# Mean and scale of seven token tiles, by DRAM and ScalarE in place of TensorE

## The chip, the cores and the metric

The kernel runs on one core of a Trainium2 chip. The metric is the device time of one execution in microseconds. Before the change it is 1456.57 us, the median of three runs (1456.12 to 1456.83).

Five engines work side by side, each through its own instructions in order: TensorE (PE in the profile; PEld is its weight load), VectorE (DVE), ScalarE (ACT), GpSimd (POOL), and SyncE (SP), which issues most of the DMAs. An engine that waits for a semaphore holds up everything behind it in its own queue.

## The reference

The input x is 2048 tokens of 576 features. It is normalized (layer norm without weights), and the normalized tokens go through a linear attention of 32 heads of 18 features and through a gated feed-forward part of 4608 features; the two results are multiplied and added to x.

```python
xn = layernorm(x)                                  # (x - mean) / sqrt(var + 1e-5)
q, k, v = heads(xn @ wqkv)
phi = lambda t: where(t > 0, t + 1, exp(t)) + 1e-6
kv, z = einsum("bhsd,bhse->bhde", phi(k), v), einsum("bhsd->bhd", phi(k))
num, den = einsum(phi(q), kv), einsum(phi(q), z) + 1e-6
s = (num / den) @ wo
b = (gelu(xn @ w_gate) * (xn @ w_up)) @ w_down
out = x + s * silu(b)
```

Everything is float32.

## The kernel before, in words

**Words.** A float32 product is made of passes over "words": an operand is held as an upper part (float32 rounded by a ScalarE copy) and a lower part (what is left, a VectorE subtraction), and TensorE multiplies the parts that matter. So every operand costs ScalarE a copy and VectorE a subtraction (`to_operand`).

**Tiles.** The 2048 tokens are 16 tiles of 128. The features of a tile lie across the partitions for the projections, so the tokens lie along a row. Tiles 0 to 3 are transposed on TensorE. For tiles 4 to 15 the host gives x already transposed beside x as it is (`load_x`), and only mean and scale, which are worked out with one token to a partition, have to be brought into rows.

**Mean and scale.** `spread` takes the moments of two tiles (VectorE, with a logarithm and an exponential on ScalarE) and `scales` finishes the scale; the result is a column of 128 numbers, one to a partition. `turn` (line 208) makes rows of them: two transposes on TensorE (L214 in the profile, out `ms`) of a column that is repeated 128 times, so that each of the 128 partitions of a PSUM bank holds the 128 means, and beside them the 128 scales. `normalize` (line 228) subtracts and multiplies on VectorE with these rows as the second operand (`x<-x,ms`, `xf_B<-x,ms`) and calls `to_operand` (`xo_B`). `place` calls `normalize` for these tiles.

**The k and v stage.** `kv_tile(t)` (line 492) does one tile: three projections `x_mm(t, 0..2)` of 14 matmuls each into banks `kv`; `k_post(t, 0)` and `k_post(t, 1)` form phi(k) (`e_k`, `pk`: two VectorE operations each, then an exponential on ScalarE and an addition on GpSimd); `v_post` copies v on ScalarE (`va`) with a column of ones that GpSimd sets. Between them stand the turn and the place of the next tile: after `x_mm(t, 0)` the turn, then `k_post(t, 0)`, `x_mm(t, 1)`, the place, `k_post(t, 1)`. At even tiles `kv_pair(t)` comes behind `x_mm(t, 0)`: the products of phi(k) and v of the two tiles before, added into one PSUM bank (`kv_a`), 40 matmuls in five groups of heads, of which four have 72 columns and the fifth 36.

**The order.** All instructions are pinned to the order in which the program writes them (`keep_in_program_order`), each on its engine. Tiles 0 to 7 come first, then the q projections of the first 1024 tokens (`q_store`, with short pieces of other work between them from the table `behind`), then tiles 8 to 15, then the rest of q (table `ahead`), the attention's output, and last the feed-forward part, which takes most of the span. Among the pieces of other work are the sums `T1` to `T4` of x operands for the feed-forward part, which `form` cuts into words and stores: the fourth stands at the end of tile 9. The statistics of tiles 12 and 13 are worked out at the end of tile 10, those of 14 and 15 at the end of tile 12.

**Buffers.** Small SBUF tiles of 2 KB a partition come from a ring of six (`gl`), PSUM banks from a ring of six (`one`); `pk` and `va` of two tiles fill a ring of four (`h`).

Of the kernel before, what the change touches and what calls it, by code (L numbers as in the profile page):

```python
# [8 lines left out]
F32 = mybir.dt.float32  # L9
# [82 lines left out]
def block_kernel(ctx, tc, x, xe, xt, wq_d, wkv_d, wo, wgu_d, wd_d, out):  # L92
# [32 lines left out]
    def vec(op, *args, **kw):  # L125
        pin(getattr(nc.vector, op)(*args, **kw))  # L126
# [58 lines left out]
    def scales(n0):  # L185

        n, mv, st = mom.pop(n0)
        v, r, c = (st[:, i, 0:n] for i in range(1, 4))
        if n == 1:
            vec("tensor_scalar", c, r, r, -0.5, op0=ALU.mult, op1=ALU.mult)  # L190
            vec("tensor_scalar", c, c, v, 1.5, op0=ALU.mult, op1=ALU.add)
            vec("tensor_scalar", c, c, r, None, op0=ALU.mult)
        else:
            vec("scalar_tensor_tensor", c, r, -0.5, r, op0=ALU.mult, op1=ALU.mult)
            vec("tensor_mul", c, c, v)
            vec("scalar_tensor_tensor", c, c, 1.5, r, op0=ALU.add, op1=ALU.mult)
        for t in range(n):
            scale_of[n0 + t] = mv[:, t, 0:1], c[:, t : t + 1]

    def center(n):  # L200

        if n >= TT:
            return
        xs = xstat[n // 2][:, n % 2]
        m, r = scale_of.pop(n)
        vec("tensor_scalar", xs, xs, m, r, op0=ALU.subtract, op1=ALU.mult)

    def turn(n, new=bank):

        xs = xstat[n // 2][:, n % 2]  # L210
        if n >= TT:
            xts[n] = t = bank(f"ms_{n}")
            for i, v in enumerate(scale_of.pop(n)):
                pin(nc.tensor.transpose(  # L214
                    t[:, i * P : (i + 1) * P], v.to_broadcast([P, P]), ident
                ))
            return
        tiles = [new(f"xt_{n}_{j}") for j in range(2)]
        xts[n] = [t[:, 0 : 3 * P].rearrange("p (k t) -> p k t", k=3) for t in tiles]
        for j in range(2):  # L220
            for k in range(3):
                pin(nc.tensor.transpose(xts[n][j][:, k, :], xs[:, j, k * P : (k + 1) * P], ident))
# [4 lines left out]

    def normalize(n, s, b, c):

        ms = xts.pop(n)  # L230
        xs = xstat[n // 2][:, n % 2, D:].rearrange("p (k t) -> p k t", k=6)
        m, r = (ms[:, None, i * P : (i + 1) * P] for i in range(2))
        vec("tensor_sub", xs, xs, m.to_broadcast([P, 6, P]))
        for j, nm in enumerate(BS[b]):
            if nm not in xo[s]:
                xo[s][nm] = big(2 * b + j, [P, 5, TBN], F32R, f"xo_{s}_{nm}")
                new_plain(s, nm)
            vec(
                "tensor_mul", xf[s][nm][:, :, c], xs[:, 3 * j : 3 * j + 3],
                r.to_broadcast([P, 3, P]),  # L240
            )
        for nm in BS[b]:
            to_operand(xo[s][nm], xf[s][nm], c)
# [32 lines left out]
        if last:  # L276
            xts.pop(n)

    mom, scale_of, xts = {}, {}, {}

    def to_operand(o, src, c):
        act(o[:, 0:3, c], src[:, :, c], AF.Copy)
# [9 lines left out]
    def difference(s, i):  # L292
        f = xf[s]
        nm, a, b, o = SUMS[i]
        vec("tensor_sub", f[o], f[a], f[b])
        f[nm] = f[o]
# [96 lines left out]
        act(e, e, AF.Exp, scale=-1.0)  # L393
        pool("tensor_add", o, o, e)

    def kv_mm(t):
        if t == 0:
            acc.append(own_bank("kv_a"))
        pk, va = pks.pop(t), vas.pop(t)
        for gi, wdt in enumerate(WIDTHS):  # L400
            for half in range(2):
                o, cs = kv_out(gi, half)
                mm(
                    o, va[:, 2 * gi + half, 0 : o.shape[0]],
                    pk[:, gi * GW + cs.start : gi * GW + cs.stop],
                    start=(t == 0 and gi == 0), stop=(t == S // P - 1),
                    skip_group_check=True,
                )
# [8 lines left out]
    def x_mm(t, c, js=(0, 1), passes=KV_PASSES):  # L417

        tb, i = divmod(t, TT)
        s, b = divmod(tb, 2)  # L420
        begin = (t, c) not in pkv
        if begin:
            pkv[t, c] = bank(f"kv_{t}_{c}")
        o = pkv[t, c]
        for j in js:
            for n, (wi, xi) in enumerate(passes):
                mm(
                    o[:, 0 : TW[c]], xo[s][BS[b][j]][:, xi, i * P : (i + 1) * P], kv_part(c, j, wi),
                    start=(begin and j == 0 and n == 0), stop=(j == 1 and (wi, xi) == (2, 2)),
                )  # L430
# [61 lines left out]
    def kv_tile(t, mid_=(), end=()):  # L492

        ahead = t % (2 * TT) != 2 * TT - 1
        x_mm(t, 0)
        if t % 2 == 0:
            kv_pair(t)
        if ahead:
            turn(t + 1)
        k_post(t, 0)  # L500
        x_mm(t, 1)
        if ahead:
            place(t + 1)
            save(t + 1)
        run(list(mid_))
        k_post(t, 1)
        v_post(t, 1)
        x_mm(t, 2)
        run(list(end))
        v_post(t, 2)  # L510

    def kv_pair(t):

        for i in (t - 2, t - 1):
            if i in vas:
                kv_mm(i)

    ph, ph_d = {}, {}

# [20 lines left out]
    def q_store(tb, gi):  # L540
        if tb not in ph_d:
            ph_d[tb] = dr.tile([P, NHG, TBN], F32, name=f"phd_{tb}")
        o = gl_tile([P, TBN], f"ph_{tb}_{gi}")
        q_mm(tb, gi, o)
        dma(out=ph_d[tb][:, gi, :], in_=o)
# [929 lines left out]
    def form(nm):  # L1475
        keep(0, nm, build(0, nm, 12))

    def form_apart(nm):
# [11 lines left out]
        dma(out=d[:, 2], in_=last[:, 0].bitcast(F32))  # L1490

    behind = {
        (0, 0): [lambda: kv_pair(N0), lambda: spread(N0, 2), lambda: difference(0, 3)],
        (0, 1): [
            lambda: scales(N0), lambda: form("T1"), lambda: q_store(1, 4),
        ],
        (0, 2): [lambda: form_apart("T3")],
        (0, 3): [lambda: turn(N0)],
        (1, 0): [lambda: place(N0)],
        (1, 1): [lambda: form("T2"), lambda: spread(N0 + 2, 2), lambda: scales(N0 + 2)],  # L1500
    }
    for tb in range(2):
        for gi in range(NHG - 1):
# [1 line left out]
            run(behind.get((tb, gi), []))  # L1505
    for n in range(N0, 2 * N0):
        ends = []
        if n < 2 * N0 - 2:
            ends.append(lambda n=n: center(n + 2) if n == N0 else x_next(n + 2))
        if n == N0 + 1:  # L1510
            ends.append(lambda: form("T4"))
        if n == 2 * N0 - 3:
            ends.append(load_wo)
        if n == 2 * N0 - 2:
            ends.append(make_sel)
        if n == 2 * N0 - 1:
            ends += [lambda i=i: difference(1, i) for i in range(3)]
        kv_tile(n, end=ends)
        if n in (N0, N0 + 2):
            load_x(n + 4, 2)  # L1520
    ahead = {
        (2, 0): [lambda: kv_pair(2 * N0), kv_done, spread_sel, lambda: difference(1, 3)],
        (2, 1): [lambda: kv_wo(4), lambda: q_hold(2, 7, 4)],
        (2, 2): [lambda: kv_wo(0), lambda: kv_wo(1), move_rows],
        (2, 3): [lambda: kv_wo(2), lambda: kv_wo(3)],
        (3, 0): [lambda: den(2), lambda: q_hold(3, 8, 4)],
# [117 lines left out]
```

## Time and profile before

| | |
|---|---|
| median of three runs | 1456.57 us |
| the profiled execution, its own time | 1456.24 us |
| its span in the profile | 1454.5 us |
| instructions | 22180 |
| VectorE busy from 126 to 135 us | 8.11 of 9 us |
| TensorE busy from 126 to 135 us | 8.79 of 9 us |
| L214 (turns), TensorE | 24 instructions |
| wait of GpSimd's `pk` for ScalarE, 85 to 180 us | 44.4 us, 8 times |

The profile is one execution. A row of a timeline gives the start, the duration, the engine, the line, the operation with its output and inputs by name, the count, and in brackets the idle time before it with what ended it. Instructions of one kind that follow each other are merged into one row. L123, L126, L129, L132 and L135 are the helpers through which ScalarE, VectorE, TensorE, GpSimd and SP get nearly all instructions, so the names of the tiles tell them apart. Matmuls are pipelined: their durations overlap, and what one costs is the distance from start to start.

### The profile page before, as it was taken

The numbers are of one execution on the slowest core, as the hardware profiler recorded it, in microseconds if no ns is written. First come the engines' busy times: TensorE is split into PE (matmuls) and PEld (weight loads), VectorE is DVE, ScalarE is ACT, GpSimd is POOL, SyncE is SP. The second block draws the span as 40 slices with busy tenths as digits, with TensorE's granted clock in tenths as the row PEclk, the third lists the DMA queues.
The fourth block names the chain that finished last, engine by engine and source line by source line (L and its number), as shares of the span: only waits on it lengthen the run. The fifth ranks groups of instructions, "written<-read, shape, count | busy, mean of one in ns | idle before, by whom it ended". The sixth has DMA issues, their size and how long they took to land.

```text
span 1454.5 us, 22180 instructions
## 1 busy us (share of the span) xinstructions
PE 1447.7 (100%) x8286; PEld 1289.9 (89%) x8286; DVE 1149.5 (79%) x1605; ACT 561.3 (39%) x914; POOL 579.6 (40%) x520
## 2 busy tenths in 40 slices
PE   9999999999999999999999999999999999999998
PEld 8989989988888888888888888888889999999998
DVE  7787767376787887888777878778888978989888
ACT  6343355332222233322332232332235555545454
POOL 3342340235756567566475755667632000000000
PEclk9999999999999999999999999999999999999999
DMA  5543105521422315224242243323389887767886
GB/s 223 191 190 141 38 30 212 209 109 51 169 98 104 130 51 182 94 94 140 72 159 87 98 149 106 113 85 118 129 277 349 262 263 251 249 188 232 278 289 224
DMA packets 118085, 233.98 MB, mean 161 GB/s; under 512 B 11018, under 2 KB 44682, under 8 KB 116058
## 3 DMA queue, kind: packets, MB, share of 16 engines
q1 hardware_dynamic: 115178, 220.31, 45.0%
q0 software_dynamic: 2656, 12.06, 2.2%
q8 instruction: 65, 1.06, 0.3%
q14 instruction: 42, 0.34, 0.1%
q10 hardware_dynamic: 144, 0.20, 0.0%
HBM read 149.91 MB, written 82.58 MB: 160 GB/s over the span
## 4 chain that ended last, share of the span: by engine, by line
PE 98%; DVE 1%; ACT 0%; issue 0%; POOL 0%; DVEq 0%; ACTq 0%; POOLq 0%
PE bd L129 25%; PE al L859 16%; PE de L859 16%; PE ga L859 16%; PE kv L129 8%; PE be L859 8%; PE s L129 4%; PE q L129 4%; PE kv_a L129 1%; PE idle L129 0%; PE d L129 0%; PE kw L129 0%; PE b L129 0%; PE ms L214 0%; DVE acc L126 0%
## 5 line engine op out<-in xcount | busy, mean ns | idle before, releaser
L132 POOL TENSOR_TENSOR sm<-raw 128x384 f32<-128x384 f32 x72 | 75.2, 1044 | 145.9 <-DMA raw<-in_wgu_dram 120.6
L129 PE MATMUL kv<-wkv,xo_B 128*128 128x412 f32 (+2 forms) x662 | 125.7, 348 | 0.0
L129 PEld LDWEIGHTS kv<-wkv,xo_B 128*128 128x128 f32 x662 | 119.8, 188 | 1.4 <-DVE wkv L126 0.5
L126 DVE TENSOR_TENSOR wa<-sm,wa 128x768 fp32r<-128x768 f32 x72 | 92.3, 1282 | 36.1 <-ACT wa L123 35.2
L129 PE MATMUL bd<-w_head,hi 128*128 128x288 f32 x516 | 117.9, 294 | 0.0
L126 DVE TENSOR_TENSOR wb<-raw,wb 128x256 fp32r<-128x256 f32 (+1 forms) x108 | 102.1, 946 | 7.4 <-ACT wb L123 5.8
L126 DVE TENSOR_TENSOR wa<-raw,wa 128x256 fp32r<-128x256 f32 x72 | 66.3, 921 | 51.7 <-ACT wa L123 50.6
L123 ACT ACTIVATE hi<-raw_h 128x1024 fp32r<-128x1024 f32 x59 | 62.5, 1060 | 94.8 <-PE bd L129 64.8
L129 PE MATMUL bd<-w_end,hi 128*128 128x288 f32 x448 | 89.8, 294 | 0.0
L123 ACT ACTIVATE spot_h<-spot_h 128x512 f32<-128x512 f32 x49 | 30.7, 633 | 150.3 <-DVE spot_h L126 150.3
L129 PEld LDWEIGHTS bd<-w_head,hi 128*128 128x128 f32 x516 | 87.0, 188 | 0.1
L126 DVE TENSOR_TENSOR raw_h<-raw_h,hi 128x1024 fp32r<-128x1024 f32 x59 | 71.7, 1220 | 17.3 <-ACT hi L123 17.2
L129 PE MATMUL bd<-w_end,raw_h 128*128 128x288 f32 x264 | 77.9, 295 | 0.0
L123 ACT ACTIVATE wa<-sm 128x1152 fp32r<-128x1152 f32 x36 | 41.8, 1161 | 91.8 <-PE de L859 91.8
L123 ACT ACTIVATE u<-al 128x512 f32<-128x512 f32 x72 | 40.9, 593 | 89.5 <-PE al L859 56.3
L129 PEld LDWEIGHTS bd<-w_end,hi 128*128 128x128 f32 x448 | 71.9, 188 | 0.0
L129 PE MATMUL bd<-beside,raw_h 128*128 128x288 f32 x240 | 70.8, 295 | 0.0
L132 POOL TENSOR_TENSOR spot_h<-spot_h,spot_h 128x512 f32<-128x512 f32 x45 | 62.7, 1399 | 2.9 <-DVE spot_h L126 2.4
L859 PE MATMUL al<-xo_B,wa 128*128 128x512 f32 x252 | 63.0, 389 | 0.0
L859 PE MATMUL al<-xr_B,wa 128*128 128x512 f32 x252 | 63.0, 389 | 0.0
L859 PE MATMUL be<-xo_T,wa 128*128 128x512 f32 x252 | 63.0, 389 | 0.0
L859 PE MATMUL be<-xr_T,wa 128*128 128x512 f32 x252 | 63.0, 389 | 0.0
(274 smaller groups left out, 4039.9 us busy)
## 6 DMA issues: line engine op xcount, KB each, us to landing
raw_h<-hs SPq DMA_DIRECT2D x176, 256.0 KB
raw<-in_wgu_dram SPq DMA_DIRECT2D x36, 768.0 KB
hs<-spot_h SPq DMA_DIRECT2D x90, 256.0 KB
hs<-spot_g SPq DMA_DIRECT2D x80, 256.0 KB
b<-in_wd_dram SPq DMA_DIRECT2D x42, 432.0 KB
hs<-spot_m SPq DMA_DIRECT2D x38, 256.0 KB
raw_g<-hs SPq DMA_DIRECT2D x22, 256.0 KB
raw_a<-hs SPq DMA_DIRECT2D x20, 256.0 KB
```

The source lines that it names most:

```text
L123: pin(nc.scalar.activation(*args, **kw))
L126: pin(getattr(nc.vector, op)(*args, **kw))
L129: pin(nc.tensor.matmul(*args, **kw))
L132: pin(getattr(nc.gpsimd, op)(*args, **kw))
L859: nc.tensor.matmul(o, w[0:rows, wi, :], xop[0:rows, xi, :], start=(start and n == 0), stop=(n == len(PASSES) - 1), skip_group_check=True,)
```

## The change

For tiles 8 to 15 `scales` now also writes the scales and the means of two tiles side by side (four numbers, 16 bytes, to a partition), stores them to DRAM, and loads them back with the whole 2 KB repeated on every partition. `sort_rows`, a ScalarE copy, brings the four numbers of a token into four rows. `normalize` takes the rows from there for tiles 9 to 15; tile 8 still takes them from a turn. Where the rows exist, `kv_tile` places the next tile right after the first projection, ahead of `k_post(t, 0)`, and makes no turn.

Three things go with it. The statistics of tiles 12 and 13 move from the end of tile 10 to the end of tile 9, those of 14 and 15 from the end of 12 to the end of 11, and the fourth form from the end of tile 9 to the end of tile 10. `kv_pair` does the wide groups of both tiles before the narrow group of both. And the q operand of group 4, which reads its small tile from the ring, comes one step earlier, twice.

```diff
@@ scales
+        if n0 >= 2 * TT:
+            vec("tensor_copy", st[:, 3, 2:4], mv[:, 0:2, 0])
+            d = dr.tile([P, 4], F32, name=f"md_{n0}")
+            mixed[n0] = g = gl_tile([P, P, 4], f"mx_{n0}")
+            dma(out=d, in_=st[:, 3, :])
+            dma(
+                out=g.rearrange("p t c -> p (t c)"),
+                in_=d.rearrange("t c -> (t c)")[None, :].to_broadcast([P, 4 * P]),
+            )
+
+    def sort_rows(n0):
+
+        g = gl_tile([P, 4, P], f"mr_{n0}")
+        act(g, mixed.pop(n0).rearrange("p t c -> p c t"), AF.Copy)
+        for t in range(2):
+            if n0 + t > 2 * TT:
+                rows_of[n0 + t] = [g[:, None, i + t] for i in (2, 0)]
@@ turn
+        if n in rows_of:
+            return
@@ normalize
-        ms = xts.pop(n)
+        if n in xts:
+            ms = xts.pop(n)
+            m, r = (ms[:, None, i * P : (i + 1) * P] for i in range(2))
+        else:
+            m, r = rows_of.pop(n)
-        m, r = (ms[:, None, i * P : (i + 1) * P] for i in range(2))
@@ kv_tile
+        early = t + 1 in rows_of
         x_mm(t, 0)
         if t % 2 == 0:
             kv_pair(t)
-        if ahead:
+        if early:
+            place(t + 1)
+        elif ahead:
             turn(t + 1)
         k_post(t, 0)
         x_mm(t, 1)
-        if ahead:
+        if ahead and not early:
             place(t + 1)
             save(t + 1)
         run(list(mid_))
         k_post(t, 1)
         v_post(t, 1)
+        if t + 2 in mixed:
+            sort_rows(t + 2)
         x_mm(t, 2)
@@ kv_pair
-        for i in (t - 2, t - 1):
-            if i in vas:
-                kv_mm(i)
+        pair = [i for i in (t - 2, t - 1) if i in vas]
+        for groups in (range(4), (4,)):
+            for i in pair:
+                kv_mm(i, groups)
+        for i in pair:
+            del pks[i], vas[i]
@@ the order of the work
-        (0, 0): [lambda: kv_pair(N0), lambda: spread(N0, 2), lambda: difference(0, 3)],
-        (0, 1): [
-            lambda: scales(N0), lambda: form("T1"), lambda: q_store(1, 4),
+        (0, 0): [
+            lambda: kv_pair(N0), lambda: q_store(1, 4), lambda: spread(N0, 2),
+            lambda: difference(0, 3),
         ],
+        (0, 1): [lambda: scales(N0), lambda: form("T1")],
...
+        (1, 2): [lambda: sort_rows(N0)],
...
-        if n < 2 * N0 - 2:
-            ends.append(lambda n=n: center(n + 2) if n == N0 else x_next(n + 2))
-        if n == N0 + 1:
+        if n in (N0, N0 + 2):
+            ends.append(lambda n=n: load_x(n + 4, 2))
+        if n in (N0 + 1, N0 + 3):
+            ends.append(lambda n=n: x_next(n + 3))
+        if n == N0 + 2:
             ends.append(lambda: form("T4"))
...
-        if n in (N0, N0 + 2):
-            load_x(n + 4, 2)
...
-        (2, 0): [lambda: kv_pair(2 * N0), kv_done, spread_sel, lambda: difference(1, 3)],
-        (2, 1): [lambda: kv_wo(4), lambda: q_hold(2, 7, 4)],
+        (2, 0): [
+            lambda: kv_pair(2 * N0), kv_done, lambda: q_hold(2, 7, 4), spread_sel,
+            lambda: difference(1, 3),
+        ],
+        (2, 1): [lambda: kv_wo(4)],
```

More of the change, by code (lines that the diff above doesn't have):

```diff
@@ L277, in save @@
             xts.pop(n)
-    mom, scale_of, xts = {}, {}, {}
+    mom, scale_of, xts, rows_of, mixed = {}, {}, {}, {}, {}
     def to_operand(o, src, c):
@@ L394, in phi, with kv_mm @@
         pool("tensor_add", o, o, e)
-    def kv_mm(t):
-        if t == 0:
+    def kv_mm(t, groups):
+        if not acc:
             acc.append(own_bank("kv_a"))
-        pk, va = pks.pop(t), vas.pop(t)
-        for gi, wdt in enumerate(WIDTHS):
+        pk, va = pks[t], vas[t]
+        for gi in groups:
             for half in range(2):
```

## The prediction, made before any run of the changed kernel

> **What bounds the kernel now.** I read the page first, then TensorE's timeline of the stage that the diff touches (85 to 180 us), then the same stretch on VectorE, ScalarE and GpSimd, because a change that takes work from TensorE is worth only what the other engines let it keep.
>
> ```profile
> span 1454.5 us, 22180 instructions
> PE 1447.7 (100%) x8286; PEld 1289.9 (89%) x8286; DVE 1149.5 (79%) x1605; ACT 561.3 (39%) x914; POOL 579.6 (40%) x520
> PE 98%; DVE 1%; ACT 0%; issue 0%; POOL 0%; DVEq 0%; ACTq 0%; POOLq 0%
> ```
>
> TensorE is busy 1447.7 of 1454.5 us and carries 98% of the chain that ended last. So an instruction taken off TensorE shortens the kernel by its issue time, as long as nothing else arrives late. TensorE's timeline around tiles 10 to 14 shows the pairs of turns (L214), the accumulations of two tiles (`kv_a`), and the projections (`kv`):
>
> ```profile
> 125.23 1.38 PE L129 MATMUL kv_a<-pk,va 128*64 128x72 f32 x40
> 126.54 0.32 PE L214 MATMUL ms<-ident,mv 128*128 128x128 f32 x1
> 126.70 0.27 PE L214 MATMUL ms<-ident,st 128*128 128x128 f32 x1
> 126.73 7.95 PE L129 MATMUL kv<-wkv,xo_B 128*128 128x412 f32 x42
> 134.52 0.27 PE L214 MATMUL ms<-ident,mv 128*128 128x128 f32 x1
> 135.54 0.32 PE L214 MATMUL ms<-ident,st 128*128 128x128 f32 x1 [0.76 <-DVE st L126]
> 135.62 7.95 PE L129 MATMUL kv<-wkv,xo_B 128*128 128x412 f32 x42
> 143.50 1.38 PE L129 MATMUL kv_a<-pk,va 128*64 128x72 f32 x40
> ```
>
> A turn between two projections, from the same timeline in a narrower window:
>
> ```profile
> 152.79 0.27 PE L214 MATMUL ms<-ident,mv 128*128 128x128 f32 x1
> 152.90 0.27 PE L214 MATMUL ms<-ident,st 128*128 128x128 f32 x1
> 152.93 0.43 PE L129 MATMUL kv<-wkv,xo_B 128*128 128x412 f32 x1
> ```
>
> Durations overlap here (columns: start, duration, engine, line, operation); what a turn costs is the distance between starts. Within the stage VectorE is nearly as full as TensorE, and its order is what the change rearranges. Its timeline for the last q operand and tile 8:
>
> ```profile
> 110.58 0.69 DVE L126 TENSOR_SCALAR ph<-q 128x512 f32<-128x512 f32 x1 [0.46 <-ACT e_q L123]
> 111.19 0.58 DVE L126 TENSOR_SCALAR e_k<-kv 128x416 f32<-128x416 f32 x1
> 111.68 0.58 DVE L126 TENSOR_SCALAR pk<-kv 128x416 f32<-128x416 f32 x1
> 112.18 0.94 DVE L126 TENSOR_TENSOR x<-x,ms 128x768 f32<-128x768 f32 x1
> 113.16 1.02 DVE L126 TENSOR_TENSOR xf_B<-x,ms 128x384 f32<-128x384 f32 x2
> 114.30 1.51 DVE L126 TENSOR_TENSOR xo_B<-xf_B,xo_B 128x256 fp32r<-128x256 f32 x4
> 115.84 0.32 DVE L126 TENSOR_SCALAR e_k<-kv 128x160 f32<-128x160 f32 x1
> ```
>
> The second k step (160 columns) of tile 9, that of tile 11, and the statistics of tiles 12 and 13 with the instruction that follows them:
>
> ```profile
> 122.23 0.33 DVE L126 TENSOR_SCALAR e_k<-kv 128x160 f32<-128x160 f32 x1
> ```
>
> ```profile
> 140.08 0.33 DVE L126 TENSOR_SCALAR e_k<-kv 128x160 f32<-128x160 f32 x1
> ```
>
> ```profile
> 132.35 0.82 DVE L126 BATCH_NORM_STATS2 bn<-x 128x6 f32<-128x288 f32 x2
> ```
>
> ```profile
> 135.41 0.58 DVE L126 TENSOR_SCALAR e_k<-kv 128x416 f32<-128x416 f32 x1
> ```
>
> From these starts: the first k step takes 1.0 us of VectorE (111.19 to 112.18), the normalization of a tile ("place") 3.66 us (112.18 to 115.84), the mean and scale of two tiles 3.06 us (132.35 to 135.41).
>
> **What is removed.** Seven pairs of turns go, for tiles 9 to 15. One that stands between projections (9, 10, 14) costs the 0.14 us from its first start to the next projection (152.79 to 152.93), and the slower first projection after it.
>
> ```profile
> L129 PE MATMUL kv<-wkv,xo_B 128*128 128x412 f32 x112 | 22.8, 354 | 0.0
> ```
>
> The mean of such a projection is 0.35, against 0.43 here: 0.08 more, 0.22 in all. A turn behind `kv_a` (11, 13, 15) costs 0.19 (126.54 to 126.73), because the slower first projection stays. Tile 12's costs 134.52 to 135.62 and the 0.08, 1.18 us, because the second turn waits 0.76 us for VectorE's scale. The sum is 3 x 0.22 + 3 x 0.19 + 1.18 = 2.4 us. The regrouped `kv_a` enters the narrow groups once in a pair instead of twice; no row shows what one entry costs. I bound it by nothing and by two of a pair's forty instructions (1.38 / 40 = 0.035 each), and take one, 0.03, so 0.2 us in eight pairs. Moving the four transposes of q operand 4 one step earlier moves the same instructions: nothing. If nobody is late, TensorE gains **2.65 us**.
>
> **What is added.** Four small VectorE copies (nearest rows: `st` operations of 0.16, so 0.1 to 0.2 each), four `sort_rows` copies on ScalarE of 128x512 elements, and on SP four stores of 2 KB and four loads of 256 KB. The load waits on SP for the store to land, and later SP work queues behind it. Its other entries in this stage are stores and x loads, and no wait quoted here ends with one of these, so I put SP at nothing.
>
> A transfer of 256 KB in this kernel, from issue on SP to last packet (slices of 0.2 us from 84.0; the packets lie in slices 13 to 16, so they end by 87.4):
>
> ```profile
> 85.79 4.67 SPq L135 DMA_DIRECT2D phd<-ph  x2
> ```
>
> ```profile
> GB/s 0 0 0 0 0 82 0 0 0 0 0 0 0 317 399 420 174 0 0 0 0 0 0 0 0 0 0 0 0 0 0 0 0 0 72 358 440 379 62 0
> ```
>
> 1.6 us, so the two in a row take some 3.5 us with the wait between them (an estimate; the nearest row that has a landing time is 4.1 us, of another queue, which makes 8.2).
>
> For `sort_rows` the nearest row is ScalarE's other 512-element pass, 590 ns; at half the rate it would be the 1045 ns of 1024 elements. I take 0.59.
>
> ```profile
> L123 ACT ACTIVATE e_q<-q 128x512 f32<-128x512 f32 x9 | 5.3, 590 | 5.4 <-PE q L129 5.4
> L123 ACT ACTIVATE xo_T<-xf_B 128x1024 fp32r<-128x1024 f32 x1 | 1.0, 1045 | 0.0
> ```
>
> ```profile
> hs<-spot_h POOLq DMA_DIRECT2D x12, 256.0 KB, 4.1
> ```
>
> `sort_rows` reads one word in every 16 bytes, which no ScalarE row here does. The Trainium skill (SBUF — State Buffer, Specifications (TRN2)) says that SBUF has 16-byte lines, that two hits on a line are needed for full bandwidth and that each crossing to a new line costs something; no run shown here bears on it.
>
> **What is moved, and what is late next.** Tile t+1 is now normalized ahead of tile t's k steps. Tile t's `pk` is therefore ready later, since the 3.66 us of a place now stand ahead of all its k steps and not between the first and the second, and `kv_a` of an even tile waits for the `pk` and `va` of the odd tile before it. From the second k step (e_k of 160 columns) to both being ready takes 2.67 us: 115.84 to the end of the memset at 118.51.
>
> ```profile
> 116.26 0.69 ACT L123 ACTIVATE e_k<-e_k 128x576 f32<-128x576 f32 x1 [1.53 <-DVE e_k L126]
> 116.85 0.76 ACT L123 ACTIVATE va<-kv 128x252 f32<-128x252 f32 x3
> ```
>
> ```profile
> 123.50 1.48 ACT L123 ACTIVATE xo_T<-xf_B 128x1536 fp32r<-128x1536 f32 x1
> ```
>
> ```profile
> 125.01 1.92 DVE L126 TENSOR_TENSOR xo_T<-xf_B,xo_T 128x1024 fp32r<-128x1024 f32 x2 [2.23 <-ACT xo_T L123]
> ```
>
> ```profile
> 118.39 0.12 POOL L132 MEMSET va<- 128x10 f32 x1
> ```
>
> A second effect: mean and scale used to be read from PSUM (`ms`); now they come from SBUF, so the subtraction and the two products read SBUF twice. VectorE operations with two SBUF inputs and GpSimd's additions shut each other out in this trace. The second of three equal differences takes 2.88 against 1.76 us, 1.1 more, beside an addition of GpSimd that takes 2.46:
>
> ```profile
> 77.26 1.76 DVE L126 TENSOR_TENSOR xf_B<-xf_B,xf_B 128x1536 f32<-128x1536 f32 x1
> ```
>
> ```profile
> 79.05 2.88 DVE L126 TENSOR_TENSOR xf_B<-xf_B,xf_B 128x1536 f32<-128x1536 f32 x1
> ```
>
> ```profile
> 77.85 2.46 POOL L132 TENSOR_TENSOR pk<-pk,e_k 128x576 f32<-128x576 f32 x1 [0.95 <-ACT e_k L123]
> ```
>
> ```profile
> L126 DVE TENSOR_TENSOR x<-x,ms x12: 941/954/956, 40.0 to 162.6; 128x768 f32<-128x768 f32 x12
> ```
>
> The subtraction from PSUM (last row: shortest, median and longest of twelve, in ns) is never slowed, though the one at 112.18 lies beside GpSimd's addition.
>
> Now the queue, on the clock of before. `sort_rows` of tiles 8 and 9 stands on ScalarE ahead of the e_q that VectorE's 110.58 waits for: 111.1. Place(9) starts at 111.7, meets GpSimd's last `ph` addition (+1.0), and ends at 116.4; TensorE waits some 0.6 us for tile 9's operand, later swallowed. The second k step of tile 8 is at 117.4. ScalarE follows with exponential (117.8), one `va` copy (118.4), `sort_rows` of 10 and 11 (118.75 to 119.35). Place(10) starts at 119.4, loses 0.5 to GpSimd's addition, and the second k step of tile 9 falls at 119.4 + 0.5 + 3.66 + 1.0 = 124.6, against 122.23. Ready at 127.3; TensorE wants tile 9 at 125.3 (125.23 + 0.6 of tile 8, less 0.5 gained). **It idles**, and is then 1.4 us behind before.
>
> Next: the statistics of tile 12, now here, 125.15 to 128.3; place(11) to 132.0; second k step of tile 10 at 133.0; on ScalarE the exponential at 133.4, `va`, `sort_rows` of 12 and 13 at 134.3, the fourth form's upper words 134.9 to 136.3; VectorE's lower words to 138.3 (1.95); place(12) to 141.95; second k step of tile 11 at 142.95 instead of 140.08. Ready at 145.6, where before began tile 11's accumulation at 143.50 + 0.6 = 144.1. So everything gained ahead of this point is lost, and 1.5 us more. Behind it VectorE has slack, and turns 13 to 15 (0.60) and three pairs (0.1) are kept: 1.5 - 0.7 = **+0.8 to 0.9 us**. The profiled execution took 1456.24 (its span and 1.74 around it), 0.33 under the median; on the median that is **1457.4**, its own range 1456.2 to 1458.6 for 0.3 us of error at each of the steps.
>
> **The rivals.**
> - *The full gain.* VectorE isn't late, because some wait that I add up (ScalarE's order, the clash with GpSimd) doesn't come. For it: 2.9 us of the walk are waits, not work. Against it: the margin of tile 11 in before is only 1.35 us (ready 142.75, wanted 144.1), less than the 1.8 us by which TensorE comes sooner. 1456.57 - 2.65 = 1453.9.
> - *No clash.* If operands with a stride of nought leave GpSimd alone, 1.5 us of the walk go and tile 11 is ready at 144.1, as before: the last 0.7 remain, 1455.9.
> - *Sorting at half rate*, each word read by itself: `sort_rows` takes 1.05 instead of 0.59 us, on the path three times, but once covered by the clash: +0.9, so 1458.3. The Trainium skill's rule of lines (SBUF — State Buffer) points this way.
> - *Slower by more: ScalarE held at `sort_rows` of tile 12.* It stands ahead of the fourth form, which stands ahead of place(12). It decides from the point at which store and load take over 6.0 us (128.3 to 134.3); every microsecond beyond is one at `kv_a` of tile 11. At 8.2 us it is +2.2: 1459.6.
> - That the turns stay is excluded: the code returns ahead of them.
>
> **How the numbers follow.** Forecast 0.42, full gain 0.22, no clash 0.15, half rate 0.11, held 0.10. What a measurement can tell from no change is about 0.2%, 2.9 us: below 1453.7 or above 1459.5. The full gain misses that bound narrowly (0.05 beyond it, for error in its sum); of the held case and the forecast's tail 0.10 lie above. So faster 0.05, same 0.85, slower 0.10. The range runs from the full gain, 1453.8, to 1459.0 between half rate and held.
>
> **What would show it.** Right: L214 has 10 turns instead of 24; `kv_a` around 127 and 145 us waits for GpSimd or VectorE; VectorE's subtraction takes over 1.3 us beside GpSimd's additions; the profile's starts around 160 lie some 1 to 1.5 us later than before. Wrong: no idle ahead of `kv_a` (full gain), subtractions of 0.95 throughout (no clash), `sort_rows` near 1 us, or ScalarE waiting for a DMA ahead of it.

## The result, and the profile after the change

The changed kernel takes **1460.58 us** (median of seven executions, 1460.44 to 1464.23) where the kernel before takes 1456.57 on the same chip (seven executions, 1455.94 to 1458.10). The ratio is 1.0033, with a 95% interval from 1.0021 to 1.0045: slower by 4.0 us. The forecast was 1457.4, and its range ended at 1459.0. The execution that was profiled took 1460.58 itself; its span is 4.3 us longer than that of before. Three of the seven executions took 1462.1 to 1464.2 and four 1460.4 to 1460.6; no record here says why.

The page of the changed kernel, its span, its busy times, and the first line of the chain that ended last:

```profile
span 1458.8 us, 22167 instructions
...
PE 1448.0 (99%) x8272; PEld 1289.4 (88%) x8272; DVE 1149.4 (79%) x1609; ACT 566.7 (39%) x918; POOL 579.9 (40%) x520
...
PE 86%; DVE 3%; POOL 1%; DMA 1%; ACT 1%; issue 1%; ACTq 0%; DVEq 0%; SPq 0%; POOLq 0%
```

TensorE issues 14 instructions fewer, as it should (ten of the 24 transposes of L214 are left, which are five turns; where the prediction speaks of 10 and 24 turns it means these instructions), and is busy for the same 1448 us; what grew is its idle time. In the chain it falls from 98% to 86%, because the chain now leaves it for VectorE, GpSimd, ScalarE and the DMAs: it passes through the load of tiles 12 and 13, which ends at about 136 us, and comes back to TensorE at 149.2. The view of waits, TensorE between 85 and 190 us of the changed kernel (in total, how often, the longest):

```profile
PE kv_a L129 <- POOL va L132: 2.6, 2, 1.6
PE kv L129 <- ACT xo_B L123: 1.1, 2, 0.8
PE kv_a L129 <- ACT va L123: 0.7, 2, 0.4
```

Before the change there was one wait in this stage, the 0.76 us of tile 12's turn. Now there are six, of 4.4 us together. TensorE's timeline of the changed kernel shows where:

```profile
115.61 10.65 PE L129 MATMUL kv<-wkv,xo_B 128*128 128x416 f32 x56 [0.81 <-ACT xo_B L123]
126.18 0.72 PE L129 MATMUL kv_a<-pk,va 128*64 128x72 f32 x16
127.90 0.47 PE L129 MATMUL kv_a<-pk,va 128*64 128x72 f32 x8 [0.99 <-POOL va L132]
128.73 0.61 PE L129 MATMUL kv_a<-pk,va 128*64 128x72 f32 x16 [0.37 <-ACT va L123]
...
142.65 2.92 PE L129 MATMUL kv<-wkv,xo_B 128*128 128x416 f32 x14 [0.29 <-ACT xo_B L123]
...
147.84 0.47 PE L129 MATMUL kv_a<-pk,va 128*64 128x72 f32 x8 [1.62 <-POOL va L132]
148.62 0.61 PE L129 MATMUL kv_a<-pk,va 128*64 128x72 f32 x16 [0.31 <-ACT va L123]
149.16 15.67 PE L129 MATMUL kv<-wkv,xo_B 128*128 128x412 f32 x84
```

The first wait is for the operand of tile 9, the fifth row's for that of tile 12. The other four stand inside `kv_a` of the pairs 8/9 and 10/11: 16 matmuls go through, then TensorE waits for the `pk` and `va` of the odd tile, does 8, and waits again, for the last two `va` copies, before the other 16. Behind the last of them the next projections, from the second of tile 12 on, start at 149.16 where they started at 145.00.

VectorE's timeline of the changed kernel, the rows that set these waits:

```profile
111.88 0.69 DVE L126 TENSOR_SCALAR ph<-q 128x512 f32<-128x512 f32 x1 [1.49 <-POOL ph L132]
...
113.47 2.00 DVE L126 TENSOR_TENSOR xf_B<-x,mr 128x384 f32<-128x384 f32 x2
...
118.13 0.31 DVE L126 TENSOR_SCALAR e_k<-kv 128x160 f32<-128x160 f32 x1
...
120.54 1.01 DVE L126 TENSOR_TENSOR x<-x,mr 128x768 f32<-128x768 f32 x1 [1.87 <-ACT mr L123]
...
125.28 0.31 DVE L126 TENSOR_SCALAR e_k<-kv 128x160 f32<-128x160 f32 x1
...
133.66 0.31 DVE L126 TENSOR_SCALAR e_k<-kv 128x160 f32<-128x160 f32 x1
...
138.53 1.92 DVE L126 TENSOR_TENSOR xo_T<-xf_B,xo_T 128x1024 fp32r<-128x1024 f32 x2 [4.33 <-ACT xo_T L123]
140.49 0.96 DVE L126 TENSOR_TENSOR x<-x,mr 128x768 f32<-128x768 f32 x1
...
145.17 0.31 DVE L126 TENSOR_SCALAR e_k<-kv 128x160 f32<-128x160 f32 x1
```

The two products of tile 9 at 113.47 take 2.00 us (1.02 before). The row at 111.88 names GpSimd, whose addition to `ph` had just ended, at 111.82; but the same instruction of VectorE waits for ScalarE's exponential `e_q` before the change and in experiment 2, and here `e_q` comes behind `sort_rows` and ends at 111.79. So this wait too goes back to ScalarE's order. Place(10) waits for the sorted rows (`mr`), and the fourth form's subtraction at 138.53 waits 4.33 us for ScalarE. The second k steps (160 columns) of tiles 8, 9, 10 and 11 start at 118.13, 125.28, 133.66 and 145.17. ScalarE, same kernel:

```profile
110.19 1.11 ACT L123 ACTIVATE mr<-mx 128x512 f32<-128x512 f32 x1
...
127.88 0.30 ACT L123 ACTIVATE st<-mv,eps_t 128x2 f32<-128x2 f32 x1 [1.29 <-DVE mv L126]
...
128.32 0.49 ACT L123 ACTIVATE va<-kv 128x252 f32<-128x252 f32 x2
...
136.01 1.11 ACT L123 ACTIVATE mr<-mx 128x512 f32<-128x512 f32 x1 [0.98 <-DMA mx<-md]
137.02 1.48 ACT L123 ACTIVATE xo_T<-xf_B 128x1536 fp32r<-128x1536 f32 x1
```

`sort_rows` takes 1.11 us, not 0.59, and the one of tiles 12 and 13 waits 0.98 us for its load; the fourth form's copy (137.02) stands behind it. And at 127.88 the logarithm of the statistics waits for VectorE, with two `va` copies behind it. The store and the load of tiles 12 and 13 on SP's queue:

```profile
129.10 0.34 SPq L135 DMA_DIRECT2D md<-st  x1
130.65 0.34 SPq L135 DMA_DIRECT2D mx<-md  x1
```

The load arrives at 136.01, where ScalarE's wait ends: 6.9 us behind the store's issue.

### The profile page after: what moved, and what is told of

Its sections match the earlier page's. It is cut to its first block, busy times and chain, and to the rows that moved or that the text cites. A ratio compares the mean times of both kernels' runs of the same rounds, so it can differ in the third digit from the quotient of the medians.

```text
span 1458.8 us, 22167 instructions
## 1 busy us (share of the span) xinstructions
PE 1448.0 (99%) x8272; PEld 1289.4 (88%) x8272; DVE 1149.4 (79%) x1609; ACT 566.7 (39%) x918; POOL 579.9 (40%) x520
## 4 chain that ended last, share of the span: by engine, by line
PE 86%; DVE 3%; POOL 1%; DMA 1%; ACT 1%; issue 1%; ACTq 0%; DVEq 0%; SPq 0%; POOLq 0%
PE bd L129 25%; PE ga L889 15%; PE de L889 15%; PE al L889 15%; PE be L889 7%; PE s L129 4%; PE kv L129 2%; PE q L129 2%; POOL spot_h L132 0%; DMA hs<-spot_g 0%; DMA mx<-md 0%; PE d L129 0%; PE kw L129 0%; PE b L129 0%; POOL spot_g L132 0%
## 5 line engine op out<-in xcount | busy, mean ns | idle before, releaser
L889 PE MATMUL ga<-xo_B,wb 128*128 128x512 f32 x252 | 63.1, 390 | 0.4 <-DVE u L126 0.4
```

The lines of the kernel that those rows point to most:

```text
L889: nc.tensor.matmul(o, w[0:rows, wi, :], xop[0:rows, xi, :], start=(start and n == 0), stop=(n == len(PASSES) - 1), skip_group_check=True,)
```

## The experiments

**My theory** after the traces: the spreading itself is nearly harmless, and the time goes into three waits on a chain that VectorE and ScalarE share: the place ahead of the k steps, ScalarE's sorting (its length, and its wait for the load) ahead of urgent work, and the last `va` copy behind the statistics. **The rivals**: the clash of VectorE with GpSimd explains most of it; the sorting, by its length, does; or the part of the change that has nothing to do with the rows (the regrouped `kv_a`, the moved q step) does. Differences below are of medians, against the kernel before on the same chip (1457.01 in the first four, 1456.71 in the next four, 1457.00 in the last four); the ratios weigh all executions and can differ from them a little.

### 1. Rows that cost nothing

Nothing is stored, loaded or sorted; the rows are those of a constant.

```diff
-            (the copy, the store and the load)
+            mixed[n0] = None
-                rows_of[n0 + t] = [g[:, None, i + t] for i in (2, 0)]
+                rows_of[n0 + t] = [ident[:, None, :]] * 2
```

> Leaves out the spreading: no copy, no store, no load, no sort_rows; place takes the rows of a constant tile in SBUF, so the output isn't the reference's. The order of the work is that of the changed kernel. Theory (the loss is queueing on ScalarE and VectorE behind sort_rows and its load): sort_rows of 1.11 us is gone three times and the 0.98 us wait for the load with it; the clash with GpSimd stays and so do the statistics ahead of the last va copy, so kv_a still waits a little around 126 and 144 us; about 1456.3, 4 us under the changed kernel. Rival (the regrouped kv_a and the moved pieces cost the time): stays at 1460 to 1461.

Measured: 1456.70, ratio 0.9997 [0.9988, 1.0005], 0.3 under before. Spreading and sorting are worth 4.3 us of the loss. But even rows that cost nothing make nothing faster. TensorE's timeline of this kernel:

```profile
126.33 0.47 PE L129 MATMUL kv_a<-pk,va 128*64 128x72 f32 x8 [0.32 <-POOL va L132]
127.08 0.61 PE L129 MATMUL kv_a<-pk,va 128*64 128x72 f32 x16 [0.29 <-ACT va L123]
...
144.81 0.61 PE L129 MATMUL kv_a<-pk,va 128*64 128x72 f32 x16 [0.28 <-ACT va L123]
```

Three waits are left, of 0.9 us; two end with the `va` copy. So the order and the clash, which are still in this kernel, take back what the removed turns bring, but make no loss by themselves. On VectorE the clash stands as in the changed kernel: 2.01 us for the two products of tile 9, and 2.14 for those of tile 10:

```profile
118.83 2.14 DVE L126 TENSOR_TENSOR xf_B<-x,ident 128x384 f32<-128x384 f32 x2
```

### 2. Sorted rows in PSUM

```diff
-        g = gl_tile([P, 4, P], f"mr_{n0}")
+        g = bank(f"mr_{n0}").rearrange("p (c t) -> p c t", c=4)
```

> sort_rows writes its rows into a PSUM bank, so that VectorE's subtraction and products have one SBUF input. Theory: place of tile 9 loses the 1.0 us that it waits for GpSimd (its two products 1.02 instead of 2.00 us), and the chain behind shifts by as much, to 1459.5. Rival (operands of two SBUF inputs don't matter on the path): 1460.6; a bank that is missed elsewhere: above 1460.6.

Measured: 1460.48, ratio 1.0024 [1.0014, 1.0034], so 0.5 us better than the change against its own runs of before, less than the intervals tell apart. The time is the rival's 1460.6 and not the theory's 1459.5. In the trace the clash is gone: the two products of tile 9 take 1.02 us, and TensorE's longest wait, in the pair 10/11, ends at 146.56 instead of 147.84, 1.3 us earlier. The profiled execution gave that back in another place. Two rows of its TensorE timeline, and a row of the view by stretches (the stretch and its length; busy us and count of PE, PEld, DVE, ACT, POOL; granted clock; DMA share; GB/s):

```profile
146.56 0.47 PE L129 MATMUL kv_a<-pk,va 128*64 128x72 f32 x8 [1.64 <-POOL va L132]
...
148.15 16.98 PE L129 MATMUL kv<-wkv,xo_B 128*128 128x412 f32 x84
```

```profile
148.15:150.90 2.75, 2.75 (x12) 2.67 (x9) 2.53 (x6) 0.99 (x2) 0.00 (x0) 0.50 0.03 1
```

The granted clock is 0.50 for 3.4 us behind the idle time, from 147.5 to 150.9 (the row shows the last 2.75), and the 84 projections take 16.98 us where the changed kernel's take 15.67 (its row at 149.16). The clash is real and its size is as I had it, but it isn't most of the loss.

### 3. Sorting by the store

The store writes the four numbers of a token into four rows of DRAM, 512 packets of 4 bytes, and ScalarE sorts nothing.

```diff
-            d = dr.tile([P, 4], F32, name=f"md_{n0}")
+            d = dr.tile([4, P], F32, name=f"md_{n0}")
-            dma(out=d, in_=st[:, 3, :])
+            dma(out=d.rearrange("c t -> t c"), in_=st[:, 3, :])
```

> The store to DRAM writes the four rows already sorted (512 packets of 4 bytes instead of 128 of 16), the load brings them to every partition, and there is no sort_rows. Theory: ScalarE's 1.11 us goes three times and the fourth form is no longer held by the load, so nearly as e1, 1456.5; place of tile 12 has until about 136 us for its rows. Rival (store and load are the cost, whoever waits): VectorE waits for the load ahead of place, 1459 to 1461.

Measured: 1478.89, ratio 1.0152 [1.0139, 1.0165], 21.9 us slower than before. **Every theory missed.** SP's timeline for the pair of tiles 8 and 9:

```profile
115.78 0.37 SPq L135 DMA_DIRECT2D md<-st  x1
126.07 0.32 SPq L135 DMA_DIRECT2D mr<-md  x1
```

The load waits on SP for the store, and that now takes 10.3 us from the store's issue to the load's. Over the four pairs it takes 8.8 to 10.9 us, where the changed kernel takes 1.5 to 3.0 (1.55 for the pair shown above, from 129.10 to 130.65). The rows come too late at every pair, and the operands with them (waits of TensorE, 85 to 190 us):

```profile
PE kv L129 <- ACT xo_B L123: 12.9, 4, 6.4
```

All waits of TensorE in this stage make 15.2 us of the 21.9. Behind them the granted clock is 0.50 in four stretches, of 20.5 us together, and matmuls there take longer. The run says nothing on ScalarE's sorting, but it shows how steep the loss is once the rows are late.

### 4. The place back between the k steps

```diff
-        if early:
-            place(t + 1)
-        elif ahead:
+        if ahead and not early:
             turn(t + 1)
...
-        if ahead and not early:
+        if ahead:
             place(t + 1)
```

> Place goes back behind the second projection, so that the first k step stands ahead of it on VectorE, as before; the rows still come by DRAM and sort_rows. Theory: the first k step of tile 9 fills VectorE's wait for sort_rows (1.87 us idle ahead of place 10), and the second k steps of tiles 9 and 11 come 1.0 us sooner: 1459.5. Rival (order of place and k steps is the main cause, since a place stands ahead of both k steps): 1457 or less.

Measured: 1459.01, ratio 1.0014 [1.0005, 1.0022], 2.0 over before: half of the loss goes with one move of the order, near the 1459.5 of the theory and not the 1457 of the rival. `kv_a` of the pair 8/9 no longer waits at all; the pair 10/11 still does, for 0.96 us. The place of tile 9 has become the tighter one:

```profile
115.98 10.65 PE L129 MATMUL kv<-wkv,xo_B 128*128 128x416 f32 x56 [1.21 <-ACT xo_B L123]
```

### 5. The last `va` copy of odd tiles ahead of the statistics

```diff
-        run(list(end))
-        v_post(t, 2)
+        if t > 2 * TT and t % 2:
+            v_post(t, 2)
+            run(list(end))
+        else:
+            run(list(end))
+            v_post(t, 2)
```

> The changed kernel, but at tiles 9, 11, 13 and 15 the last va copies stand ahead of the statistics and not behind them. Theory: kv_a of tiles 10 and 12 no longer waits the 0.37 and 0.31 us for va behind the logarithm; about 0.3 to 0.6 us under the changed kernel. Rival (the wait for pk covers it): no difference.

Measured: 1460.21, ratio 1.0023 [1.0014, 1.0032]. That is 0.5 us better than the change, as expected, but less than the intervals tell apart. The two waits for `va` are gone from TensorE's timeline, but a part of it is lost again, since the operand of tile 12 comes later instead (1.00 in place of 0.29):

```profile
142.69 2.91 PE L129 MATMUL kv<-wkv,xo_B 128*128 128x416 f32 x14 [1.00 <-ACT xo_B L123]
```

One wait mended alone is mostly paid at the next.

### 6. The order alone, without the rows

The kernel before, with the regrouped `kv_a` and the q step moved as in the change, and the turns kept.

```diff
+        for groups in (range(4), (4,)):
+            for i in pair:
+                kv_mm(i, groups)
...
+            lambda: kv_pair(N0), lambda: q_store(1, 4), lambda: spread(N0, 2),
```

> The kernel before with two parts of the change alone: the groups of kv_a regrouped, and the q operand of group 4 one step earlier, twice. Theory: 0.2 us faster than before, so no difference that can be measured. Rival (the moved pieces cost the time): 2 us or more slower than before.

Measured: 1457.06, ratio 1.0001 [0.9992, 1.001]: no difference. A pair of `kv_a` goes from 1.38 to 1.36 us. So the rival falls for these two parts. The moved statistics, the moved fourth form and the x loads behind them are not in this run; no run takes them alone.

### 7. Sorting without the stride, a load that doesn't wait

The load takes 128 different rows of x and waits for no store, and ScalarE's copy reads its 512 words in a row.

```diff
-                in_=d.rearrange("t c -> (t c)")[None, :].to_broadcast([P, 4 * P]),
+                in_=x[n0 * P : (n0 + 1) * P, 0 : 4 * P],
...
-        act(g, mixed.pop(n0).rearrange("p t c -> p c t"), AF.Copy)
+        act(g, mixed.pop(n0).rearrange("p t c -> p (t c)").rearrange("p (c t) -> p c t", c=4), AF.Copy)
```

> The changed kernel, but the load of 256 KB takes 128 different rows of x from DRAM in place of one row of 2 KB repeated, so it does not wait for the store, and sort_rows reads its 512 words in a row: other values, so the output isn't the reference's. Theory: packets of the load take about 84 ns as those of the q stores, not 200 to 300; sort_rows takes 0.59 and not 1.11 us; ScalarE doesn't wait ahead of the second-to-last sort_rows; in all some 2 us under the changed kernel. Rival (the 16 bytes are not the reason, and the load is slow for the x load beside it): 1.11 us and 3 us stay.

Measured: 1458.66, ratio 1.0013 [1.0004, 1.0022], 1.95 over before and so 2.1 better than the change. The group of sorting copies in this kernel:

```profile
L123 ACT ACTIVATE mr<-mx 128x512 f32<-128x512 f32 x4 | 2.5, 621 | 0.0
```

621 ns for the same 512 words in a row, where the changed kernel's group has 1115. No copy waits for a DMA. So the length of the sorting and the late load are worth half of the loss while order and clash stay. That doesn't make order and clash the other half: in experiment 1 they stay too, and nothing is lost. What one of the parts costs depends on which others are there.

### 8. All of it mended

The place late again (4), the rows in PSUM (2), the last `va` copy of odd tiles ahead of the statistics (5), and two sortings moved behind the work that they held up:

```diff
-        if t + 2 in mixed:
+        if t + 2 in mixed and t != 2 * TT + 2:
             sort_rows(t + 2)
...
-        (1, 2): [lambda: sort_rows(N0)],
+        (1, 3): [lambda: sort_rows(N0)],
...
-            ends.append(lambda: form("T4"))
+            ends += [lambda: form("T4"), lambda n=n: sort_rows(n + 2)]
```

> The changed kernel with the causes of the theory mended together: place behind the second projection as before, the rows in PSUM, sort_rows of tile 8 behind the last q operand, that of tile 12 behind the fourth form, and the va copies of odd tiles ahead of the statistics. Theory: TensorE waits under 0.5 us at kv_a of tiles 10 and 12, and the gain of 2.65 us less at most 1 us is left: 1.6 to 2.6 us faster than before. Rival (the rows by DRAM can't be had without TensorE waiting): as before or slower.

Measured: **1454.66**, ratio 0.9984 [0.9975, 0.9993], 2.05 us faster than before and 6.1 better than the change. It beats both kernels. One wait of TensorE is left between 85 and 190 us:

```profile
142.79 0.86 PE L129 MATMUL kv_a<-pk,va 128*64 128x72 f32 x24 [0.17 <-POOL va L132]
```

On ScalarE the fourth form comes first, and the sorting of tiles 12 and 13 behind it finds its load there (no wait in brackets). It still takes 1.10 us; it holds nobody now:

```profile
131.84 1.48 ACT L123 ACTIVATE xo_T<-xf_B 128x1536 fp32r<-128x1536 f32 x1
133.21 1.10 ACT L123 ACTIVATE mr<-mx 128x512 f32<-128x512 f32 x1
```

This version and the changed kernel issue the same 8272 matmuls in the same order, so their starts can be laid side by side. The distance grows by 1.0 us at tile 9's operand, by 1.7 in the pair 8/9, 0.6 at tile 12's operand and 1.9 in the pair 10/11 (5.4 in the stage, for the six waits above, with some 0.15 of refilling each), then by 0.7 at 498 us, where a `ga` matmul waits for VectorE. The last also stands in the profile of experiment 6 (0.7), whose time is that of before; I count it to the execution and not to the change.

### 9 to 12. The mended version, with one mend taken back

Each of the four differs from version 8 by one mend (number 12 by two).

```diff
(9)  +        g = gl_tile([P, 4, P], f"mr_{n0}")
(10) +        if early:
     +            place(t + 1)
(11) +        if t + 2 in mixed:
     +            sort_rows(t + 2)
(12) +        run(list(end))
     +        v_post(t, 2)
     +        (1, 2): [lambda: sort_rows(N0)],
```

> The mended version with the rows back in SBUF, all else as there. If the clash between VectorE's operations on two SBUF inputs and GpSimd's additions costs the kernel time by itself, the places of tiles 9 to 12 last some 1.0 us longer and the kernel is 0.5 to 1.0 us slower than the mended version's 2.05 us below the kernel before: 1.05 to 1.55 us below. Rival: with the order mended VectorE has that much slack in this stage and the clash is swallowed: 1.9 to 2.2 below.

> The mended version with the place of the next tile ahead of the k steps again. If the earlier place costs by itself (the second k step 2.7 us later, as the first experiment with the late place had it at 1.6 us of 3.6), the kernel stands 0.4 to 1.0 us below the one before instead of 2.05. Rival: the earlier place only hurt because sorting and the clash came on top of it; then it stays 1.9 to 2.2 below.

> The mended version with the sorting of tile 12 ahead of the fourth form again. If ScalarE's wait for the load (about 1 us) and the 1.1 us of sorting ahead of the fourth form push place(12) and the k steps behind it, the kernel stands 0.3 to 1.0 us below the one before instead of 2.05 (1.1 to 1.8 us lost). Rival: the place of tile 12 comes late enough behind the fourth form to swallow it: 1.9 to 2.2 below.

> The mended version with the last va copy of odd tiles behind the statistics' logarithm again and the sorting of tile 8 back ahead of the last q operand. If the va copy behind the logarithm is a wait of its own at kv_a, 0.3 us at two to three pairs come back: 1.1 to 1.7 us below the kernel before instead of 2.05. Rival: VectorE's order hides both: 1.9 to 2.2 below.

| version | median us | ratio to before, interval | against before | TensorE's waits, 85 to 190 us |
|---|---|---|---|---|
| 8: mended | 1454.66 | 0.9984 [0.9975, 0.9993] | -2.05 | 0.2 |
| 9: rows in SBUF | 1455.47 | 0.9987 [0.9978, 0.9995] | -1.53 | 0.5 |
| 10: place early | 1456.40 | 0.9996 [0.9987, 1.0004] | -0.60 | 1.6 |
| 11: sorting ahead of the fourth form | 1456.66 | 0.9997 [0.9989, 1.0006] | -0.34 | 2.0 |
| 12: `va` last, sorting of tile 8 early | 1456.45 | 0.9995 [0.9986, 1.0004] | -0.55 | 1.3 |
| the change | 1460.58 | 1.0033 [1.0021, 1.0045] | +4.01 | 4.4 |

The intervals of 10, 11 and 12 still overlap that of 8 a little; that these are real prices rests on the last column, where each wait taken back shows, in its place. Number 9, the clash alone: one place, one wait.

```profile
112.56 1.39 DVE L126 TENSOR_TENSOR x<-x,mr 128x768 f32<-128x768 f32 x1
```

```profile
115.15 10.65 PE L129 MATMUL kv<-wkv,xo_B 128*128 128x416 f32 x56 [0.30 <-ACT xo_B L123]
```

The subtraction takes 1.39 instead of 0.95 us, and the operand of tile 9 is 0.30 late. Half a microsecond in the median, which the runs can't tell from nothing; the expected value was at the edge. Number 10, the place ahead of the k steps, on TensorE, within what was expected:

```profile
127.34 0.86 PE L129 MATMUL kv_a<-pk,va 128*64 128x72 f32 x24 [0.99 <-POOL va L132]
...
145.12 0.86 PE L129 MATMUL kv_a<-pk,va 128*64 128x72 f32 x24 [0.62 <-POOL va L132]
```

Number 11, on ScalarE and on TensorE, as expected:

```profile
133.01 1.09 ACT L123 ACTIVATE mr<-mx 128x512 f32<-128x512 f32 x1 [1.03 <-DMA mx<-md]
```

```profile
140.76 2.92 PE L129 MATMUL kv<-wkv,xo_B 128*128 128x416 f32 x14 [1.39 <-ACT xo_B L123]
...
144.97 0.86 PE L129 MATMUL kv_a<-pk,va 128*64 128x72 f32 x24 [0.64 <-POOL va L132]
```

The wait for the load (1.03) and the sorting (1.09) make 2.1 us ahead of the fourth form, and 1.39 and 0.64 of them arrive at TensorE. Number 12, on TensorE, costs more than was expected (1.5 against 0.35 to 0.95), because the sorting of tile 8 ahead of the last q operand makes tile 9 late, which the expectation gave no weight:

```profile
115.52 10.62 PE L129 MATMUL kv<-wkv,xo_B 128*128 128x416 f32 x56 [0.78 <-ACT xo_B L123]
...
143.94 0.47 PE L129 MATMUL kv_a<-pk,va 128*64 128x72 f32 x8 [0.21 <-POOL va L132]
144.70 0.61 PE L129 MATMUL kv_a<-pk,va 128*64 128x72 f32 x16 [0.29 <-ACT va L123]
```

The four prices, 0.5, 1.45, 1.7 and 1.5, add up to 5.2 of the 6.1 us between version 8 and the change. What is left is within their errors.

## Why the prediction was wrong, step by step

The method held, a walk along VectorE's and ScalarE's queue to the second k step of tile 11, and so did its finding that this tile gives back what the turns bring. What failed are two durations and one instruction that it left out, in the parts "What is added" and "What is moved".

- **What is removed: right.** The sum gave 2.65 us if nobody is late. Version 8 gains 2.1 us between 87 and 188 us (its distance to before goes from +0.20 to -1.92): 0.2 for each of five turns and 1.2 for that of tile 12, as summed, less its one wait with refilling (0.2) and 0.1 at tile 9's operand.
- **The regrouped `kv_a`: right**, 0.03 a pair against 0.02 in experiment 6, and not to be measured in the whole.
- **`sort_rows` at 0.59: wrong, 1.11 us.** I took the row with the same number of elements and gave the half rate, 1.05, a chance of 0.11 as a rival. Experiment 7 shows that it is the stride. The rule of the Trainium skill on 16-byte lines (SBUF — State Buffer, Specifications (TRN2)) pointed the right way, and the trace agrees: 1.115 us with a step of 16 bytes, 0.621 without.
- **Store and load at 3.5 us: wrong, 6.9.** The rival "held" had the mechanism and its point of decision: above 6.0 us ScalarE waits ahead of the fourth form. It did, for 0.98. In the walk `sort_rows` of tile 12 was to end at 134.9; it ended at 137.1.
- **Not in the walk at all: the last `va` copies of an odd tile** stand on ScalarE behind the logarithm of the statistics, which the change had moved to odd tiles, and that waits for VectorE. I counted the statistics' 3.06 us on VectorE and not their instructions on ScalarE. `kv_a` waits 0.37 and 0.31 for it.
- **The place ahead of the k steps: right** in mechanism and place. From the second k step of tile 11 to `pk` and `va` the walk had 2.67 us; the trace has 145.17 to 147.84, 2.67. Versions 4 and 10 price the order at 2.0 and 1.45 us.
- **The clash: right in part.** Place(9) lost the 1.0 us that was forecast, in the products and not in the subtraction; place(10) lost 0.07 and not 0.5. The Trainium skill (SBUF — State Buffer, Who interferes with whom) says that a VectorE instruction with two SBUF inputs contends with a GpSimd instruction that reads SBUF, and one with a single SBUF input does not; here, 2.00 us with the rows in SBUF against 1.02 with the rows in PSUM. Its price in the mended order is about 0.5 us (experiment 9).

The walk in numbers, second k steps of tiles 8, 9, 10 and 11: forecast 117.4, 124.6, 133.0, 142.95; measured 118.13, 125.28, 133.66, 145.17. Up to tile 10 it is 0.7 late, of which 0.4 lies in this execution from its start (TensorE's instructions at 84 us are that much behind those of before). From there it is another 1.5: the 0.98 of the wait and the 0.52 of the longer sorting. With the 0.5 that the late `va` copy adds in the pair 10/11 that is 0.3 + 1.5 + 0.5 = 2.3 us over the forecast; the stage lost 3.2 (from +0.41 at 84 us to +3.64 at 188) where the sum said 0.85. The other 1.0 of this execution's longer span lies at its start (0.4) and at 498 us (0.7); which part of that is in the median stays open.

The rivals were listed as if one excluded the others. Half rate, the held ScalarE and the clash came together, and a chain adds them. That is why the range, which was cut at 1459.0 between two rivals, was too narrow: the half rate's 0.9 and the held ScalarE's 2.2 (for 8.2 us), both priced in the prediction, would have brought 1457.4 to 1460.5 if added. Two of its signs of being wrong came, a `sort_rows` of about 1 us and a ScalarE that waits for a DMA ahead of one; the sign that it set for the clash, a subtraction above 1.3 us, did not (0.95 to 1.07), as the clash lay in the products. And the later starts around 160 us came 3.9 to 4.2 us late, not 1 to 1.5.

## What to carry to other kernels

Work that is taken off a full engine and given to one with time to spare still enters that engine's queue at a place, and everything behind it there is moved: list the instructions behind each inserted one, on each engine, and ask which of them the full engine waits for next. An insertion that waits for a DMA goes behind the urgent work, not ahead of it; here the same copies, moved behind what they held up, with the place and the `va` copies put back in order, turned +4.0 us into -2.05. And where several bounds of a forecast lie on one chain, add their bad ends before the range is drawn.

## What the runs showed of the hardware

**A wide load is slow to start and slow at first.** The view by stretches of the changed kernel, behind the load's issue at 130.65 (last two columns: DMA share and GB/s):

```profile
130.65:132.40 1.75, 1.75 (x12) 1.75 (x11) 1.53 (x5) 0.91 (x2) 0.00 (x0) 1.00 0.00 0
132.40:134.20 1.80, 1.80 (x12) 1.80 (x11) 1.77 (x5) 0.13 (x1) 0.00 (x0) 1.00 0.76 85
134.20:136.00 1.80, 1.80 (x12) 1.79 (x11) 0.00 (x1) 0.83 (x2) 1.11 (x1) 1.00 0.94 284
```

Nothing moves for 1.75 us; then the engines are 76% busy for 85 GB/s. All 128 packets of 2 KB read the same 2 KB of DRAM. Their median time is 209 ns at tile 12 (192 in version 8), and 84 with the different rows of x in experiment 7, whose mean is no shorter (304 against 249, for a few very slow ones). That does not make the repeated row the cause. The load of tiles 14 and 15 repeats a row too, with no other load issued behind it until 166 us: from its issue to its last packet it takes 3.0 us in the changed kernel and in version 8, where that of tiles 12 and 13, with loads of x behind it in the queue, takes 4.85 and 4.0, and its packets have medians of 176 and 81 ns. The different rows of experiment 7 take 4.8 us at tile 12 and 4.3 at tile 14. So a repeated row is not always slow, and why the load of tile 12 takes longer stays open.

**Stores of 4 bytes**: 512 of them hold the waiting load for 8.8 to 10.9 us in the four pairs of experiment 3, 128 stores of 16 bytes for 1.5 to 3.0 in the changed kernel. For tiles 8 and 9 the records of the 4-byte packets themselves end 1.9 us behind the issue; what the rest is spent on no trace here shows.

**Short waits can cost clock, by where they fall.** In the profile of experiment 2 the granted clock fell to 0.50 for 3.4 us behind TensorE's waits of 1.64 and 0.31 us; in the changed kernel's profile, with waits of 1.62 and 0.31 at the same place, it stayed at 1.00. The Trainium skill (TensorE: Matmul & The Clock Gate, Part 1) gives half the clock as the state behind an idle window of about 3.4 us; the half and the length agree, but TensorE was not idle throughout the window here. In the fourteen profiles the stretches at half clock inside a kernel last 3.41 us or 6.83, and they begin on a grid of 3.41 us. Laid over the matmuls, that grid sorts the cases: behind the five stretches at full clock in which TensorE was busy for 43% or less (one in experiment 2, from 144.1 to 147.5, and four in experiment 3, at 3 to 43%) the clock fell to 0.50, and behind all others, busy for 60% or more, it stayed at 1.00. In experiment 2 the two waits fell into one such stretch, in the changed kernel into two (64% and 79% busy). That is read from the traces; no run was made to test it.
